# Splitting each attention head's 64 dimensions into even and odd ones instead of lower and upper halves, in a fused attention and maxout kernel

## The chip, the cores and the metric

The kernel runs on one core of one Trainium2 chip. The metric is the device time of one execution in microseconds (us), the median of several. A core has a matrix engine (PE, whose weight loads are listed apart as PEld), a vector engine (DVE), a scalar engine for activation functions (ACT), a general engine (POOL) and a sync engine (SP), which here does nothing but issue transfers. Sixteen DMA engines carry the transfers of the core.

## The reference

```python
def _attn_ref(q, k, v, cap):              # q, k, v: (8, 12, 448, 64)
    scores = matmul(q, k^T) / sqrt(64)
    scores = cap * tanh(scores / cap)     # cap = 30
    attn = softmax(scores)
    return matmul(attn, v)

x = attn_out as (8 * 448 tokens, 12 * 64 = 768)
h1, h2 = x @ w1, x @ w2                   # w1, w2: (768, 1024)
return maximum(h1, h2) @ w_out            # w_out: (1024, 768), result (3584, 768) float32
```

The kernel uses maximum(h1, h2) = relu(x(w1 - w2)) + x w2. So it needs wd = w1 - w2 and the product wm = w2 w_out, and computes relu(x wd) w_out + x wm.

## The kernel before, in words

**Tiling.** 96 heads are taken two at a time ("pairs", 48 of them), and two pairs (four heads) make one step t of 24. Three pairs are one group g for loading, so there are 16 groups. For a step, the scores of each key block go to PSUM (`scores`, lines 297 and 302), ACT takes tanh (lines 303, 305) and exp (`ex`, line 310), PE sums the exponentials for the softmax's divisor (`total`), and PE multiplies them with v (`values`, lines 368 and 375). `values` makes two PSUM tiles, u = 0 and u = 1. In each, the four heads of the step stand in four blocks of 32 partitions, and each block holds one half of that head's 64 dimensions. A weight load for it takes 32 columns of `vp` or `vl` (v in bf16). `normalize` writes the two tiles as rows `2q + u` of xT, where q counts the steps of one batch, so a 128-row chunk of xT holds one half of the dimensions of four heads.

**The weights.** Rows of w1 and w2 must be in the same order as those of xT. The function `x_rows` picks the 128 rows of chunk c: in the kernel before, four blocks of 32 consecutive rows, with 32 rows skipped between blocks. `load_w2(c)` (line 210) brings chunk c of w2 from float32 to bf16 through the queue of POOL into a tile that is named gT in the profile. `load_w1(c)` (line 218) brings chunk c of w1 as float32 (512 KB) through the queue of SP into tiles that the profile names osb (c = 0 to 3) and xT (c = 4, 5). POOL subtracts one from the other (`subtract`, line 221). PE turns chunks of w2 (`turn_w2`, line 228) and multiplies them with w_out (`premultiply`, line 239; chunk 0 by `premultiply_first`, line 527).

**The order of work.** The order on every engine is written out by hand; each engine takes its own list strictly in order. On SP the list begins: k and q of groups 0 and 1, v of group 0, v of group 1, k and q of group 2, w1 chunks 0 and 1, the transposing transfer `cross(2)`, w1 chunks 2 to 5, k and q of group 3, v of group 2, `cross(3)`, and then the later groups. `cross(g)` (line 275) turns the bf16 copies of k and q (kqf) into qkT, which `scores` needs from group 2 on; it has to wait for POOL's casts of that group's k and q (lines 177 to 189). Groups 0 and 1 are turned by PE (`transposes`).

POOL's list in the same stretch: issue w2 chunks 0 and 1 and the four w_out loads (line 201), cast group 1, issue w2 chunks 2 to 5, cast v of groups 0 and 1 (lines 150, 154), cast k and q of group 2, subtract chunks 0 and 1, subtract chunks 2 and 3, cast k and q of group 3, subtract chunks 4 and 5, cast v of group 2.

The two MoE products of each batch (`moe`, lines 403, 415, 418) fill PE between the attention's pieces, through a list of generators from which the function `F(n)` takes n matmuls; the last of them run after the last exp.

[...]

Of the kernel before, what the change touches and what calls it, by code (L numbers as in the profile page):

```python
# [10 lines left out]
def kernel(  # L11
# [11 lines left out]
    nc = tc.nc  # L23
# [5 lines left out]
    B, H, S, D = q.shape  # L29
# [3 lines left out]
    P = 128  # L33
# [30 lines left out]
    vp = [const.tile([P, 2 * L, NJ, D], bf16, name=f"vp{i}") for i in range(2)]  # L64
    vl = [const.tile([P, L, P], bf16, name=f"vl{i}") for i in range(2)]
# [74 lines left out]
    def cast(eng, g, what, n0=0, n1=L, halves=(0, 1)):  # L140
# [53 lines left out]
    w2b = (  # L194
        xpool.tile([P, FC, 2 * S], bf16, name="gT", bufs=1)
        .rearrange("p f s -> p (f s)")[:, : KC * DF]
        .rearrange("p (c n) -> p c n", c=KC)
    )
# [5 lines left out]

    def x_rows(w, c):

        return w.rearrange("(q m u i) n -> q u m i n", m=4, u=2, i=32)[c // 2, c % 2]

    def load_w2(c):
        nc.gpsimd.dma_start(  # L210
            out=w2b[:, c, :], in_=x_rows(moe_w2, c)
        )

    w1x = xpool.tile([P, NP, 2 * S], bf16, name="xT").rearrange("p c s -> p (c s)").bitcast(f32)

    def load_w1(c):
        w1_in[c] = opool.tile([P, DF], f32, name="osb") if c < OB else w1x[:, (c - OB) * DF : (c - OB + 1) * DF]
        nc.sync.dma_start(out=w1_in[c], in_=x_rows(moe_w1, c))
# [29 lines left out]
    expo = {}  # L248
# [63 lines left out]
    def e_of(t, ab, j):  # L312
        p, m = LP[ab, j]
        return expo[t, p][:, m : m + (1 if j == NJ else 2), :]
# [45 lines left out]
    def values(t):  # L360

        out = []
        for u, bank in enumerate(("pv", "ss")):
            ps = pv_psum.tile([P, 512], f32, name=bank)
            for j in range(NJ):
                for ab, h, r in HEADS:
                    g, n = divmod(2 * t + ab, L)
                    nc.tensor.matmul(  # L368
                        ps[r, :S], vp[g % 2][:, 2 * n + h, j, 32 * u : 32 * u + 32], e_of(t, ab, j)[:, h, :],
                        start=(j == 0), stop=False,  # L370
                    )
            for ab, h, r in HEADS:
                g, n = divmod(2 * t + ab, L)
                d = 64 * h + 32 * u
                nc.tensor.matmul(
                    ps[r, :S], vl[g % 2][:, n, d : d + 32], expo[t, 2][:, ab, :], start=False, stop=True
                )
            out.append(ps)
        return out
# [107 lines left out]
    for c in range(2):  # L487
        load_w2(c)
# [21 lines left out]
    for c in range(2, KC):  # L510
        load_w2(c)
# [63 lines left out]
    total(0)  # L575
    F(3)
    normalize(0, values(0))
    F(2)

    for t in range(1, NQ):  # L580
        i = 2 * t
# [55 lines left out]
        else:  # L637
            F(12)
        normalize(t, values(t))
        if t % 3 == 2:  # L640
            fill_q.append(moe(t // 3))
# [35 lines left out]
```

## Time and profile before

| | |
|---|---|
| device time, median of three | 389.99 us (388.97 to 390.05) |
| span of the profiled execution | 388.7 us |
| PE busy | 335.2 us (86%) |
| ACT busy | 281.7 us (72%) |
| DVE busy | 235.0 us (60%) |
| POOL busy | 112.8 us (29%) |
| transfers of SP's queue | 58.21 MB, 55.8% of 16 engines' span |
| transfers of POOL's queue | 3.16 MB, 5.6% |

Busy time is the time in which an engine works on an instruction, and issuing a transfer does not count. A share of the whole span is a mean over stages with different limits: the first 90 us, in which the weights and the first groups come in, are another stage than the steady part up to about 332 us, where the last exp ends, and the tail after it, where PE alone works off the MoE. The lines of the profile are shown where the prediction reads them.

### The profile page before, as it was taken

To read this page: it belongs to the slowest core of one execution; us is meant where nothing else is said; L and a number is where in the kernel's file an instruction comes from. 1 tells how busy PE (TensorE), PEld (TensorE's weight loads), DVE (VectorE), ACT (ScalarE), POOL (GpSimd) and SP (SyncE) were. 2 spreads that over 40 slices of the span, in tenths; PEclk is the share of its full clock that TensorE was granted. 3 is DMA by queue.
4 is the path that set the end of the run, shared out by engine and by line. 5 is a ranking of instruction groups with operands and counts; after the bars stand their busy time and mean duration, and the time that the engine had idled before them with its cause. 6 is when DMAs were issued, how large, how long until landed. Compare 5 with 4: busy or idle time off the path is not lost.

```text
span 388.7 us, 6775 instructions
## 1 busy us (share of the span) xinstructions
PE 335.2 (86%) x2710; PEld 162.6 (42%) x2710; DVE 235.0 (60%) x410; ACT 281.7 (72%) x265; POOL 112.8 (29%) x154
## 2 busy tenths in 40 slices
PE   3387749108899899999999999999999999999996
PEld 1143325004345344444443454444444445455563
DVE  4144507106867786688768876788777677742421
ACT  3679839306899899999999999999999999200000
POOL 5632623174811901370173108111901100000000
PEclk9998969857999999999999999999999999999999
DMA  8999764466986857793978296399268012102022
GB/s 280 212 172 232 115 114 140 144 179 171 271 221 200 233 136 177 232 244 99 258 222 221 58 266 184 107 238 308 83 156 232 2 42 81 42 0 87 37 83 81
DMA packets 105432, 61.80 MB, mean 159 GB/s; under 512 B 64568, under 2 KB 100408, under 8 KB 105400
## 3 DMA queue, kind: packets, MB, share of 16 engines
q1 hardware_dynamic: 101144, 58.21, 55.8%
q0 software_dynamic: 4256, 3.16, 5.6%
q8 instruction: 21, 0.34, 0.4%
q14 instruction: 11, 0.09, 0.1%
HBM read 42.47 MB, written 11.01 MB: 138 GB/s over the span
## 4 chain that ended last, share of the span: by engine, by line
PE 38%; ACT 28%; SPq 11%; DVE 10%; DMA 9%; issue 2%; POOL 1%; ACTq 0%; POOLq 0%
PE mm L403 15%; ACT expo L310 14%; ACT tanh L303 12%; PE mm L418 7%; PE mm L415 5%; SPq L135 4%; DMA gT<-in_moe_w_dram 4%; PE s L302 4%; DVE esum L329 3%; ACT tanh L305 2%; DMA osb<-in_moe_w_dram 2%; DVE esum L331 2%; SPq L124 2%; SPq L129 2%; PE ss L368 2%
## 5 line engine op out<-in xcount | busy, mean ns | idle before, releaser
L303 ACT ACTIVATE tanh<-s 128x896 bf16<-128x896 f32 x144 | 124.2, 914 | 44.2 <-PE s L302 42.3
L310 ACT ACTIVATE expo<-tanh 128x1792 bf16<-128x1792 bf16 (+1 forms) x96 | 144.8, 1509 | 0.1
L418 PE MATMUL mm<-wo_sb,gT 128*128 128x384 bf16 x448 | 86.3, 327 | 0.0
L403 PE MATMUL mm<-xT,wd_sb 128*128 128x448 bf16 x384 | 79.8, 353 | 4.1 <-DVE gT L407 2.4
L302 PE MATMUL s<-qkT 64*128 64x448 bf16 x288 | 43.3, 370 | 32.3 <-DMA qkT<-kqf 26.4
L415 PE MATMUL mm<-wm_sb,xT 128*128 128x384 bf16 x336 | 66.9, 326 | 0.2 <-DVE osb L422 0.2
L157 POOL CAST vp<-vr 128x1152 bf16<-128x1152 f32 x14 | 16.4, 1171 | 141.0 <-PE ss L368 79.1
L418 PEld LDWEIGHTS <-gT 128*128 128x128 bf16 x448 | 42.1, 98 | 35.1 <-issue 8.8
L422 DVE COPY osb<-mm 128x384 f32<-128x384 f32 x56 | 31.0, 554 | 38.2 <-PE mm L418 38.0
L403 PEld LDWEIGHTS <-wd_sb 128*128 128x128 bf16 x384 | 35.9, 98 | 43.5 <-issue 12.9
L331 DVE TENSOR_TENSOR esum<-expo 128x896 bf16<-128x896 bf16 x42 | 30.3, 721 | 29.9 <-ACT expo L310 29.2
L407 DVE TENSOR_SCALAR gT<-mm 128x448 bf16<-128x448 f32 x64 | 39.6, 620 | 13.3 <-PE mm L403 13.0
L415 PEld LDWEIGHTS <-xT 128*128 128x128 bf16 x336 | 31.5, 98 | 26.3 <-issue 6.3
L329 DVE TENSOR_TENSOR esum<-esum,expo 64x896 bf16<-64x896 bf16 x42 | 32.1, 763 | 1.1
L302 PEld LDWEIGHTS <-qkT 64*128 64x128 bf16 x288 | 9.5, 95 | 55.0 <-DMA qkT<-kqf 27.0
L333 DVE TENSOR_TENSOR esum<-esum,expo 128x896 bf16<-128x896 bf16 x42 | 26.8, 638 | 0.2
L305 ACT ACTIVATE tanh<-s 128x896 bf16<-128x896 f32 x24 | 22.0, 917 | 6.5 <-PE s L297 6.0
L244 DVE CAST wm_sb<-mm 128x384 bf16<-128x384 f32 x10 | 5.6, 556 | 33.0 <-PE mm L239 33.0
L354 DVE STREAM_TRANSPOSE st<-ss 128x448 f32<-128x448 f32 x24 | 15.5, 646 | 10.0 <-PE ss L352 5.6
L177 POOL CAST kqf<-kr 128x1152 bf16<-128x1152 f32 x14 | 17.3, 1239 | 12.6 <-DMA kr<-in_k_dram 12.1
L368 PEld LDWEIGHTS <-vp 128*32 128x32 bf16 x576 | 13.3, 96 | 18.5 <-issue 10.7
L368 PE MATMUL ss<-expo,vp 128*32 128x448 bf16 x288 | 17.8, 353 | 1.2 <-DVE st L354 1.1
(69 smaller groups left out, 275.2 us busy)
## 6 DMA issues: line engine op xcount, KB each, us to landing
kr<-in_k_dram SPq DMA_DIRECT2D x14, 576.0 KB, 4.6
qr<-in_q_dram SPq DMA_DIRECT2D x14, 576.0 KB, 8.3
vr<-in_v_dram SPq DMA_DIRECT2D x14, 576.0 KB, 5.3
out_dram<-osb SPq DMA_DIRECT2D x20, 384.0 KB, 2.7
out_dram<-osb SPq DMA_DIRECT2D x16, 192.0 KB, 4.0
osb<-in_moe_w_dram SPq DMA_DIRECT2D x4, 512.0 KB
gT<-in_moe_w_dram POOLq DMA_DIRECT2D x6, 256.0 KB, 13.9
wo_sb<-in_moe_w_out_dram POOLq DMA_DIRECT2D x4, 384.0 KB, 16.2
```

The costliest lines, as they stand in the source:

```text
L302: nc.tensor.matmul(s[:, h, :S], k0[r, j * P : (j + 1) * P], qTn[r, :])
L303: nc.scalar.activation(tanh[t, p][:, 2 * m : 2 * m + 2, :], s[:, :, :S], AF.Tanh, scale=scale / cap)
L305: nc.scalar.activation(tanh[t, p][:, 0:2, :], s[:, :, :S], AF.Tanh, scale=scale / cap)
L310: nc.scalar.activation(expo[t, p], tanh[t, p][:, 0:n, :], AF.Exp, scale=float(cap))
L329: nc.vector.tensor_add(d, d, expo[t, 2][r, :, :])
L331: nc.vector.tensor_add(d, e_of(t, ab, 1 if ab else 0), e_of(t, ab, 2 if ab else 1))
L368: nc.tensor.matmul(ps[r, :S], vp[g % 2][:, 2 * n + h, j, 32 * u : 32 * u + 32], e_of(t, ab, j)[:, h, :], start=(j == 0), stop=False,)
L403: nc.tensor.matmul(ps[:, :S], wd_sb[:, c, f * P : (f + 1) * P], x[:, c, cs], start=(c == 0), stop=(c == KC - 1))
L407: nc.vector.tensor_relu(g[:, f, cs], ps[:, :S])
L415: nc.tensor.matmul(ps[:, : DM // 2], x[:, c, ts], wm_sb[:, c, hs], start=(c == 0), stop=False)
L418: nc.tensor.matmul(ps[:, : DM // 2], g[:, f, ts], wo_sb[:, f, hs], start=False, stop=(f == FC - 1))
L422: nc.vector.tensor_copy(osb[:, hs], ps[:, : DM // 2])
```

## The change

The tile u of a step now holds the dimensions u, u + 2, u + 4 ... of each head, so u = 0 takes the even and u = 1 the odd ones. Chunk c of the weights then consists of every second row of 256 consecutive rows: 128 rows with one constant step of two rows, where before there were four blocks of 32 rows. The purpose is a simpler address pattern for the loads of w1 and w2. In return the 32 columns of v that a weight load takes stand two apart. The sums, the number of instructions and their order on every engine stay what they were.

```diff
     def x_rows(w, c):
 
-        return w.rearrange("(q m u i) n -> q u m i n", m=4, u=2, i=32)[c // 2, c % 2]
+        return w.rearrange("(q p u) n -> q u p n", p=P, u=2)[c // 2, c % 2]
...
                     nc.tensor.matmul(
-                        ps[r, :S], vp[g % 2][:, 2 * n + h, j, 32 * u : 32 * u + 32], e_of(t, ab, j)[:, h, :],
+                        ps[r, :S], vp[g % 2][:, 2 * n + h, j, u::2], e_of(t, ab, j)[:, h, :],
                         start=(j == 0), stop=False,
                     )
...
-                d = 64 * h + 32 * u
                 nc.tensor.matmul(
-                    ps[r, :S], vl[g % 2][:, n, d : d + 32], expo[t, 2][:, ab, :], start=False, stop=True
+                    ps[r, :S], vl[g % 2][:, n, 64 * h + u : 64 * h + 64 : 2], expo[t, 2][:, ab, :], start=False, stop=True
                 )
```

In the built program the source of a w1 or w2 load was 4 x 32 x 1024 elements and is now 128 x 1024; the destination is 128 partitions of 1024 elements in both.

More of the change, by code (lines that the diff above doesn't have):

```diff
@@ L205, in x_rows @@
     def x_rows(w, c):
-        return w.rearrange("(q m u i) n -> q u m i n", m=4, u=2, i=32)[c // 2, c % 2]
+        return w.rearrange("(q p u) n -> q u p n", p=P, u=2)[c // 2, c % 2]
     def load_w2(c):
-        nc.gpsimd.dma_start(
-            out=w2b[:, c, :], in_=x_rows(moe_w2, c)
-        )
+        nc.gpsimd.dma_start(out=w2b[:, c, :], in_=x_rows(moe_w2, c))
     w1x = xpool.tile([P, NP, 2 * S], bf16, name="xT").rearrange("p c s -> p (c s)").bitcast(f32)
```

## The prediction

> **What bounds the kernel now.** I began with the span in 40 slices (9.7 us each), where the first 90 us look different from the rest.
>
> ```profile
> PE   3387749108899899999999999999999999999996
> ACT  3679839306899899999999999999999999200000
> ```
>
> From the tenth slice on PE is at 9 and so is ACT until the tail; before that both fall to 0 or 1 near 78 to 87 us, and sag at 10 to 20 us and 49 us. ACT's timeline gives the three holes with their lengths (last bracket: idle before, and releaser):
>
> ```profile
> 21.40 1.73 ACT L303 ACTIVATE tanh<-s 128x896 bf16<-128x896 f32 x2 [5.02 <-PE s L302]
> ...
> 54.53 1.73 ACT L303 ACTIVATE tanh<-s 128x896 bf16<-128x896 f32 x2 [7.14 <-PE s L302]
> ...
> 89.09 0.92 ACT L303 ACTIVATE tanh<-s 128x896 bf16<-128x896 f32 x1 [17.44 <-PE s L302]
> ```
>
> ACT lost 5.02 + 7.14 + 17.44 = 29.6 us to PE's scores. Next I asked the waits of the first 92 us what PE lacked (total, times, longest):
>
> ```profile
> ACT tanh L303 <- PE s L302: 37.4, 6, 17.4
> ...
> PE s L302 <- DMA qkT<-kqf: 26.4, 2, 18.7
> ...
> POOL wd_sb L221 <- DMA osb<-in_moe_w_dram: 17.7, 4, 9.0
> ...
> POOL kqf L177 <- DMA kr<-in_k_dram: 10.9, 1, 10.9
> ...
> PE mm L228 <- DMA gT<-in_moe_w_dram: 6.2, 1, 6.2
> ```
>
> Hole 1 is chunk 0 of w2 (gT, line 228); holes 2 and 3 are cross(2) and cross(3) (qkT). Behind the crosses stand w1 (osb) and k of group 3. The chain of waits of the same stretch (start, length, what) says the same: w2, w1, then SP's issues, then the last cross.
>
> ```profile
> 5.72 14.07 DMA gT<-in_moe_w_dram
> ...
> 35.63 9.13 DMA osb<-in_moe_w_dram
> ...
> 62.14 8.68 SPq L135
> ...
> 83.85 4.60 DMA qkT<-kqf
> ```
>
> Last, the busy time by windows; the last two columns are the share of the 16 DMA engines and GB/s:
>
> ```profile
> 8.00:10.00 2.00, 1.37 (x26) 0.70 (x25) 1.15 (x3) 2.00 (x3) 2.00 (x4) 1.00 1.06 401
> ...
> 40.00:43.00 3.00, 3.00 (x30) 1.84 (x31) 1.16 (x3) 2.97 (x3) 2.81 (x5) 1.00 0.26 105
> ...
> 55.00:62.00 7.00, 7.00 (x43) 3.85 (x42) 2.37 (x4) 5.92 (x6) 1.07 (x1) 0.84 0.25 100
> 67.00:70.00 3.00, 2.83 (x18) 1.40 (x16) 1.34 (x3) 2.97 (x4) 2.13 (x1) 1.00 0.26 104
> ```
>
> While w1 moves, the share is flat at 0.25 to 0.26, four engines of 16, at 100 to 105 GB/s. At 8 to 10 us, with q, k and v, all 16 worked at 401 GB/s. That plateau is the bound of the start: one 512 KB chunk takes 524 kB / 102 GB/s = 5.1 us, six take 31 us, and everything behind them on those four engines queues.
>
> [...] No strided weight load is in this trace.
>
> **The change part by part.**
>
> w1, six loads (line 218). Each goes from 5.1 us on four engines to 524 kB / about 390 GB/s (near the 401 seen) = 1.35 us, so six go from 31 to 8 us.
>
> w2, six loads (line 210). Chunk 0 was issued at 5.72 and landed at 19.8. On all engines: q, k, v of the first two groups are five loads of 672 KB, 3.44 MB, from about 2 us, hence until 10.8; two chunks of w2 read 1.05 MB, 2.7 us more, so until 13.5[...]. PE asks for it at 13.6, ACT runs dry only at 16.4. Hole 1 closes: ACT and PE move up by 5.0 us. The w_out loads (3.1 MB, 8 us) then run from 13.5 to 21.6; their first lands near 16.5 and is needed at 24.07 - 5 = 19.1, the last is needed at 31 - 5 = 26.
>
> Hole 2. All reads up to q of group 2 are 3.44 + 1.05 + 3.15 + 2.1 (w2 chunks 2 to 5) + 2.06 (v of group 1, k and q of group 2) = 11.8 MB, 30 us at 390 GB/s, so q lands near 33. POOL's last casts of that group take 1.7 us, cross(2) is issued near 36 instead of 43.04, with w1 chunks 0 and 1 (2.7 us) through. Landing costs 4.6 us, the price of the undisturbed cross at 83.85 (this one took 10.8): 40.6. PE reaches it at 46.15 - 5.0 = 41.1. The hole closes; ACT carries on at 47.4 - 5.0 = 42.4 instead of 54.53, 12.1 us earlier.
>
> Hole 3. After cross(2) leaves the engines at about 41, w1 chunks 2 to 5 need 5.4 us, k, q of group 3 another 3.6: landing at 49 and 51. POOL subtracts chunks 2 and 3 by 48 (2.13 us each), casts by 53 (3.65 us in all at 80.20 to 83.83), cross(3) lands at 53.3 + 4.6 = 57.9. PE asks at 69.8 - 12.4 = 57.4; ACT has work until 71.65 - 12.1 = 59.5, and scores take 0.6 us: 58.5. The hole closes with 1 us to spare. ACT's instruction that started at 89.09 starts at about 59.5 to 60.5, a gain of 28.6 to 29.6.
>
> After that nothing is new: the lists are the same, PE and ACT wait for no transfer after 89 us, and the next loads (v of group 3, k and q of groups 4 and 5) follow cross(3) at the same distance as before. So the shift reaches the end. After hole 3 PE ran at a granted clock of 0.50 (window 86 to 90), and ACT then waited 1.81 us at 93.4; a warm PE may return about 1 us. I book it against the risk that a hole leaves a rest.
>
> The strided weights (lines 368, 375): 576 + 192 = 768 loads.
>
> ```profile
> L368 PEld LDWEIGHTS <-vp 128*32 128x32 bf16 x576 | 13.3, 96 | 18.5 <-issue 10.7 <-POOL vp L157 0.4
> ```
>
> A load of 32 columns takes 96 ns, no less than the 98 of the 128-column ones, so 96 ns is not the reading alone; and 12 matmuls follow each other in 0.68 us, 57 ns apart, with loads beside them. Lower bound 0. Upper bound: spacing doubled, 768 x 57 ns = 44 us on PE. I take 0[...].
>
> Sum: 390.0 - 28.5 = 361.5 us.
>
> **The rivals.**
>
> A: w2 does not speed up, since its queue spreads otherwise or because its engines are full in 8 to 20 us (share above 1 there speaks for that). Hole 1 stays at 5.0, holes 2 and 3 close: 390 - 24.5 = 365.5.
>
> B: a new wait takes the old one's place. The chain cross(3) needs subtract, cast and landing in a row, and my slack is 1 us; SP's in-order issues could hold k of group 3. If hole 2 leaves 2 us and hole 3 leaves 7, the time is 361.5 + 9 = 370.5. For it: SP's issues took up to 8.68 us each. Against it: those long issues stand inside the plateau; at 89.90 one took 0.39.
>
> C, the other side: a stride halves the weight load's rate and it shows in full. Then 361.5 + 44 = 405.5, slower than before. Against it: the equal 96 and 98 ns.
>
> D: the plateau has another cause (for instance the rows themselves), loads stay as they are: 390.
>
> **How the numbers follow.** Forecast 0.64, A 0.13, B 0.16, C 0.04, D 0.03. The likeliest gives 361.5. The forecast itself may be off by some 5 us either way (holes with a rest, or the warm clock as an extra gain); A lies inside that, and to hold most of B the range goes to 371. Low end: all 29.6 and about 4 more from the warm clock and from small waits after the holes: 356. Faster by over 0.3%: forecast, A and B, 0.93; same 0.03 (D); slower 0.04 (C).
>
> **What would show it.** Right: DMA share near 1 and 350 GB/s or more while osb is filled; the first gT landing in 7 to 9 us; PE's waits for qkT under 2 us each; ACT without an idle of over 2 us after 16 us; line 368 still at 96 ns and 57 ns apart; the stretch from the first step after cross(3) to the end unchanged in length. Wrong: the plateau at a quarter persists; SP's issues at line 135 stay long; PEld of line 368 above 150 ns, or 12 of its matmuls over 1 us.

## The result, and the profile after

| | before | after |
|---|---|---|
| device time, median (four runs each) | 390.02 us | 365.02 us |
| range | 388.97 to 393.11 | 363.54 to 367.15 |
| span of the profiled execution | 388.7 us | 362.4 us |
| packets of POOL's queue | 4256 | 1952 |

The ratio is 0.9351, 95% interval 0.9278 to 0.9424. The changed kernel takes 25.0 us less. Its lines have other numbers: 300, 301 and 308 are the scores, tanh and exp, 226 and 237 `turn_w2` and `premultiply`, 210 and 216 the loads of w2 and w1, 273 the transposing transfer, 366 and 372 `values`.

The span in 40 slices (9.1 us each) of the changed kernel:

```profile
PE   3898597979999999999999999999999999999996
ACT  3989689979998999899998999999999998000000
```

The hole of two slices is gone. What is left of the three holes stands in ACT's timeline (last bracket: idle before, releaser):

```profile
20.48 1.73 ACT L301 ACTIVATE tanh<-s 128x896 bf16<-128x896 f32 x2 [0.28 <-PE s L300]
24.63 0.92 ACT L303 ACTIVATE tanh<-s 128x896 bf16<-128x896 f32 x1 [0.84 <-PE s L295]
...
44.87 1.73 ACT L301 ACTIVATE tanh<-s 128x896 bf16<-128x896 f32 x2 [3.32 <-PE s L300]
...
49.94 1.73 ACT L301 ACTIVATE tanh<-s 128x896 bf16<-128x896 f32 x2 [1.77 <-PE s L300]
...
62.86 0.92 ACT L301 ACTIVATE tanh<-s 128x896 bf16<-128x896 f32 x1 [0.19 <-PE s L300]
...
66.00 0.92 ACT L303 ACTIVATE tanh<-s 128x896 bf16<-128x896 f32 x1 [0.64 <-PE s L295]
```

The instruction that started at 89.09 starts at 62.86. From it to the end it is 388.7 - 89.09 = 299.6 us before and 362.4 - 62.86 = 299.5 after: all of the gain lies ahead of it. Hole 1 (5.02) is gone, hole 3 (17.44) is 0.19, hole 2 (7.14) is 3.32, and a short wait behind hole 2 grew from 1.08 to 1.77. Before the tanh at 24.63 ACT idles 0.84, where the kernel before has one wait of 0.81 in that stretch, at another tanh. Of the 29.6 us of the three holes, 29.6 - 3.32 - 0.28 - 0.19 - (1.77 - 1.08) - (0.84 - 0.81) = 25.1 us came back. (ACT's first tanh also started 1.1 us sooner in this profile, but it does so in a run below that has the old loads, too, so it isn't the change's.)

The waits of the first 66 us (total, times, longest), and a window in which w1 makes up nearly all that moves (last two columns: share of the 16 DMA engines, GB/s):

```profile
PE s L300 <- DMA qkT<-kqf: 5.9, 2, 4.3
...
POOL wd_sb L219 <- DMA osb<-in_moe_w_dram: 4.2, 1, 4.2
...
POOL kqf L177 <- DMA kr<-in_k_dram: 1.2, 1, 1.2
```

```profile
46.00:49.00 3.00, 3.00 (x11) 1.48 (x10) 0.56 (x1) 2.17 (x2) 1.04 (x1) 0.50 0.98 362
```

PE waited 26.4 us for qkT and waits 5.9; POOL waited 17.7 for w1 and 10.9 for k, now 4.2 and 1.2. The share in the window is 0.98 where it was 0.25, the rate 362 GB/s where it was 100. The chain of waits of that stretch names something new:

```profile
3.69 17.10 DMA vr<-in_v_dram
...
22.76 9.48 DMA vr<-in_v_dram
...
57.71 4.69 DMA qkT<-kqf
```

It no longer goes through w2 and w1 but through v of group 0, the casts that free its buffer, and v of group 1 (issued at 22.76, landed at 32.24).

### The profile page after: what moved, and what is told of

Same layout as the page of the kernel before. It is cut to its first block, busy times and chain, and to the rows that moved or that the text cites. A ratio compares the mean times of both kernels' runs of the same rounds, so it can differ in the third digit from the quotient of the medians.

```text
span 362.4 us, 6775 instructions
## 1 busy us (share of the span) xinstructions
PE 336.7 (93%) x2710; PEld 163.6 (45%) x2710; DVE 237.1 (65%) x410; ACT 281.6 (78%) x265; POOL 113.4 (31%) x154
## 2 busy tenths in 40 slices
DMA packets 103201, 61.79 MB, mean 170 GB/s; under 512 B 62337, under 2 KB 98177, under 8 KB 103169
## 3 DMA queue, kind: packets, MB, share of 16 engines
q0 software_dynamic: 1952, 3.15, 4.8%
## 4 chain that ended last, share of the span: by engine, by line
PE 39%; ACT 28%; DVE 13%; DMA 10%; SPq 4%; POOL 3%; issue 2%; ACTq 0%; POOLq 0%
PE mm L400 15%; ACT expo L308 14%; ACT tanh L301 12%; DMA vr<-in_v_dram 9%; PE mm L415 8%; PE mm L412 6%; PE s L300 3%; DVE esum L327 3%; DVE esum L329 3%; ACT tanh L303 2%; DVE esum L331 2%; PE ss L366 2%; DVE gT L404 2%; PE pv L366 2%; DVE osb L419 1%
## 5 line engine op out<-in xcount | busy, mean ns | idle before, releaser
L329 DVE TENSOR_TENSOR esum<-expo 128x896 bf16<-128x896 bf16 x42 | 31.3, 746 | 29.6 <-ACT expo L308 28.9
L327 DVE TENSOR_TENSOR esum<-esum,expo 64x896 bf16<-64x896 bf16 x42 | 30.5, 727 | 1.1
L331 DVE TENSOR_TENSOR esum<-esum,expo 128x896 bf16<-128x896 bf16 x42 | 29.1, 693 | 0.2
L177 POOL CAST kqf<-kr 128x1152 bf16<-128x1152 f32 x14 | 17.7, 1262 | 3.4 <-DMA kr<-in_k_dram 2.9
L366 PE MATMUL pv<-expo,vp 128*32 128x448 bf16 x288 | 18.1, 356 | 0.0
```

The source lines that it names most:

```text
L327: nc.vector.tensor_add(d, d, expo[t, 2][r, :, :])
L329: nc.vector.tensor_add(d, e_of(t, ab, 1 if ab else 0), e_of(t, ab, 2 if ab else 1))
L331: nc.vector.tensor_add(d, d, e_of(t, ab, 0 if ab else 2))
L366: nc.tensor.matmul(ps[r, :S], vp[g % 2][:, 2 * n + h, j, u::2], e_of(t, ab, j)[:, h, :], start=(j == 0), stop=False,)
```

## The experiments

Two of the edits are in the diff already; where an experiment's edit is short it is shown. Ratios are to the kernel before, run beside it.

**Which load brings how much.** `x_rows` of the changed kernel was used for w1 alone, or for w2 alone, with v as before.

```diff
-        nc.sync.dma_start(out=w1_in[c], in_=x_rows(moe_w1, c))
+        nc.sync.dma_start(out=w1_in[c], in_=x_rows_step(moe_w1, c))
```

> Only w1's loads take the rows in steps of two (w2, v as before, so the rows of w1 and w2 don't belong together). Theory (number of engines): w1 moves at 300 GB/s or more on 16 engines, holes 2 and 3 nearly close, hole 1 (5 us) stays as w2's first chunk still lands at 19 to 20 us: 369 to 371 us. Rival (w1 and w2 both have to be quick, the holes hang on each other): 378 us or more. Rival (w2 never mattered): 365 us.

> Only w2's loads take the rows in steps of two. Theory: first gT landing falls from 14 us to 8 us, hole 1 closes, the plateau of w1 at a quarter of the engines stays with holes 2 and 3; SP's list moves up by some 4 us: 385 to 387 us. Rival (w2 sets the whole start): under 375 us. Rival (w2's queue spreads anyway): 390 us.

Measured: w1 alone 367.70 us, ratio 0.9453 (0.9405 to 0.9501); w2 alone 386.55 us, 0.9928 (0.9892 to 0.9964). Against 389.63 beside them these are 21.9 and 3.1 us (by the intervals 19.4 to 23.2 and 1.4 to 4.2), together 25.0, which agrees with what the whole change brought. ACT's timeline with w1 alone:

```profile
19.30 1.73 ACT L307 ACTIVATE tanh<-s 128x896 bf16<-128x896 f32 x2 [3.66 <-PE s L306]
...
48.22 1.73 ACT L307 ACTIVATE tanh<-s 128x896 bf16<-128x896 f32 x2 [2.54 <-PE s L306]
```

and with w2 alone:

```profile
48.70 1.73 ACT L307 ACTIVATE tanh<-s 128x896 bf16<-128x896 f32 x2 [7.18 <-PE s L306]
...
83.66 0.92 ACT L307 ACTIVATE tanh<-s 128x896 bf16<-128x896 f32 x1 [17.50 <-PE s L306]
```

With w1 alone hole 1 stays (3.66 us) and hole 3 has no line any more; with w2 alone hole 1 has none, and holes 2 and 3 are whole. The first two loads of w2 landed a median 12.9 us after their issue with w1 alone and 8.3 with w2 alone. So each hole belongs to the load that the prediction gave it. The w1 run was 1 to 3 us quicker than its expectation said; its hole 1 was 1.3 us shorter than the 5 us put in, and the rest has no cause shown.

**The strided weights.** Only the two lines of `values` were changed.

> Only the weight loads of v take every second column; w1 and w2 are loaded as before, so the product uses rows in the wrong order. Theory (strided weight loads cost nothing): 390 us within 0.7, line 368's weight loads at 96 ns, 12 matmuls in 0.68 us. Rival (the stride costs PE time that the gain of the loads hides): 393 to 400 us.

Measured: 389.82 us, ratio 1.0001 (0.9978 to 1.0023). Group of the weight loads in this run:

```profile
L366 PEld LDWEIGHTS <-vp 128*32 128x32 bf16 x576 | 13.2, 96 | 18.5 <-issue 10.9
```

That is 96 ns, and its chain of waits has 12 of the matmuls in 0.68 us, as before. Reading every second column costs nothing that these runs can tell from their noise (0.9 us either way); the rival with 3 to 10 us is out.

**Number of engines or the rows themselves.** The rows of before, in the same blocks, but four transfers for each chunk:

```diff
-        nc.sync.dma_start(out=w1_in[c], in_=x_rows(moe_w1, c))
+        for m in range(4):
+            nc.sync.dma_start(out=w1_in[c][32 * m : 32 * m + 32, :], in_=x_rows(moe_w1, c)[m])
```

> The rows of the kernel before, in the same blocks, but each w1 chunk is four transfers of 32 rows to 32 partitions. Theory (the outer dimension of 4 sets the number of engines): each transfer runs on 16 engines, no plateau; as in the run with w1 alone, plus 18 more issues of 0.55 us on SP: 370 to 377 us. Rival (the row addresses, blocks with gaps, are slow): plateau at a quarter stays, 390 us.

Measured: 371.29 us, 0.9536 (0.9495 to 0.9576). A window of its w1 stretch:

```profile
50.00:55.00 5.00, 5.00 (x34) 2.83 (x33) 2.10 (x4) 4.01 (x5) 3.64 (x2) 0.89 1.03 239
```

The share is 1.03: the same rows, in four transfers whose outer dimension is 32, kept all 16 engines busy. The rate is only 239 GB/s, not 362, and why is open: each transfer also fills 32 partitions and not 128, and no run varied that alone. SP's issues come near as a limit, too: its timeline has eight of 131 kB in 3.67 us, which by estimate lets at most 286 GB/s through.

Then the number of blocks, with nothing else changed (`m=8, i=16` and `m=2, i=64` in `x_rows` of before):

> The kernel before with w1 and w2 taken in eight blocks of 16 rows with gaps of 16 (v as before, so the product takes rows in the wrong order). Theory (the outer dimension sets the number of engines): 8 engines, a plateau at half of the DMA engines near 205 GB/s while w1 moves alone, 2.6 us a chunk; 368 to 376 us. Rival (blocks with gaps are slow as such): the quarter stays, 390 us.

> The same with two blocks of 64 rows and gaps of 64. Theory: 2 engines, a plateau at an eighth near 51 GB/s, 10.2 us a chunk, six take 61 us; 415 to 435 us. Rival (longer blocks are better): faster than 390 us.

Measured: 374.97 us with eight (0.9618, 0.9561 to 0.9675), 420.84 with two (1.0795, 1.0759 to 1.083). Windows of the w1 stretch, eight blocks and then two:

```profile
37.00:40.00 3.00, 3.00 (x39) 1.49 (x41) 1.16 (x3) 2.97 (x3) 2.68 (x4) 1.00 0.51 199
```

```profile
66.00:78.00 12.00, 11.80 (x88) 5.71 (x92) 4.43 (x9) 8.98 (x8) 0.11 (x1) 0.76 0.13 47
```

| blocks in the source's outer dimension | share of the engines | GB/s | time, us |
|---|---|---|---|
| 2 | 0.13 | 47 | 420.8 |
| 4 (before) | 0.25 | 100 | 390.0 |
| 8 | 0.51 | 199 | 375.0 |
| 128 rows in one (after) | 0.98 | 362 | 365.0 |

The share is blocks / 16 within 0.02 (the last with 16 of 16), and the time follows. Longer blocks are worse, not better. The time column has w2 in it as well, which is loaded in the same pattern. On POOL's queue no view shows w2's share of the engines, but the waits go the same way: PE's wait for its first chunk was 9.98 us with two blocks, 6.20 with four, 1.15 with eight, and after the change PE's timeline shows none.

**What is left of hole 2.** First the changed kernel once more, as the measure of the three runs beside it:

> The changed kernel once more, as the measure for the three runs beside it: 365 us within 1.5, ACT idle of 3 us before its first tanh after the first transposing transfer (hole 2).

Measured: 363.68 us, 0.9325 (0.9288 to 0.9361). In this profile hole 2 was 1.95 and hole 3 was 2.98 us, against 3.32 and 0.19 in the first: together they came to 3.5 us in the first and 4.9 us in the second. POOL's timeline of the first profile shows what the transposing transfer (issued at 39.48) stood behind:

```profile
32.30 1.37 POOL L150 CAST vp<-vr 64x576 bf16<-64x576 f32 x2 [9.56 <-DMA vr<-in_v_dram]
...
35.84 1.14 POOL L177 CAST kqf<-kr 128x1152 bf16<-128x1152 f32 x1
```

v of group 1 landed at 32.3, its casts took until 35.8, and only then came those of k and q. So v got a second raw buffer (`bufs=2`), which lets it be issued at 4 us instead of 23:

> The changed kernel with two raw buffers for v, so that v of group 1 is issued at about 4 us and not behind the casts of group 0's v (23 us before). Theory (the rest of hole 2 is v of group 1, late because its buffer is held, and its casts ahead of those of k and q on POOL): the first transposing transfer is issued by 34 us and not at 39.5, hole 2 under 1 us, w_out a little later: 361 to 363.5 us. Rival (the engines are full until 33 us, so an earlier issue only moves others back): 365 us or more, with PE waiting for w_out.

Measured: 362.94 us, 0.9313 (0.9277 to 0.935), no different from the changed kernel. POOL's timeline:

```profile
33.81 1.14 POOL L177 CAST kqf<-kr 128x1152 bf16<-128x1152 f32 x1 [3.63 <-DMA kr<-in_k_dram]
...
36.35 1.15 POOL L177 CAST kqf<-qr 128x1152 bf16<-128x1152 f32 x1 [0.70 <-DMA qr<-in_q_dram]
```

v is out of the way, but POOL now waits for k until 33.81 and for q until 36.35; the transposing transfer went out at 38.09, 1.4 us sooner than in the first profile of the changed kernel, and hole 2 was 2.35. The time lies in the range that the theory gave, but its reason fell: the issue was to come by 34 us and hole 2 to go under 1 us. The rival's reason was the better one in part, though PE lost only 0.56 us to w_out. k of group 2 was issued at 8.24, 15 us sooner than in the changed kernel (23.22), and still came only at 33.8. In the changed kernel all 16 engines are busy in that stretch (a share of 1.03 to 1.16 in every 2 us from 10 to 34 us): here the bytes ahead counted more than the time of issue. For q there is a second possible reason, which no run tells from the first: SP's two issues before it took 13.2 us, so it was itself issued only at 21.98.

```profile
8.65 13.22 SPq L135 DMA_DIRECT2D kr<-in_k_dram  x2
21.98 2.81 SPq L124 DMA_DIRECT2D qr<-in_q_dram  x1
```

The next runs take 1 MB out of the front (w2 chunks 4 and 5 are first used near 49 us); the second of them also loads and casts k and q of group 2 ahead of v of group 1:

```diff
-    for c in range(2, KC):
+    for c in range(2, 4):
         load_w2(c)
...
     cast(nc.gpsimd, 2, "k")
     cast(nc.gpsimd, 2, "q")
+    for c in range(4, KC):
+        load_w2(c)
```

> The changed kernel with w2 chunks 4 and 5 issued after POOL's casts of group 2 (about 39 us and not 18), 1 MB less on the engines in front of v of group 1 and k, q of group 2. Theory (transfers in front are what delays v of group 1): it lands 2 to 2.5 us sooner, hole 2 shrinks by as much: 362 to 363.5 us. Rival (that landing is set by its late issue alone): 365 us.

> As the run with late w2 chunks, and also k and q of group 2 loaded and cast before v of group 1. Theory: the first transposing transfer waits only for k and q, is issued near 30 us and lands long before PE asks; but v of group 1 is cast later, and the values of step 1 may wait for it by up to 3 us: 361 to 364 us. Rival (w_out, which shares the engines with the earlier k and q, arrives late and costs PE more than hole 2): 366 us or more.

Measured: 368.45 us (0.9445, 0.9413 to 0.9478) and 367.59 us (0.9452, 0.9411 to 0.9494), both slower than the changed kernel. Both forecasts of a gain were missed. In the run with late w2 chunks alone the theory held as far as it went: v of group 1 was cast from 28.53, and the transfer issued at 35.71, 3.8 us sooner. But then, in PE's timeline of the run with late w2 chunks:

```profile
50.59 0.93 PE L300 MATMUL s<-qkT 64*128 64x448 bf16 x4 [9.90 <-DMA qkT<-kqf]
```

and its DMA issues from 35 us on (issue to landing):

```profile
gT<-in_moe_w_dram POOLq DMA_DIRECT2D x2, 256.0 KB, 9.3
...
qkT<-kqf SPq DMA_TRANSPOSE x1, 14.8
```

The transposing transfer took 14.8 us (15.6 in the other run) beside the two w2 loads, and 4.7 in the changed kernel. (The other run's 367.59 lies where its rival put it, but w_out cost PE only 1.8 us there, against 9.2 for qkT.) To test that these two are what slowed it, they were moved behind it, and w1 chunks 4 and 5 behind k and q of group 3:

```diff
             subtract(0, nc.gpsimd)
             subtract(1, nc.gpsimd)
+            for c in range(4, KC):
+                load_w2(c)
...
-    for c in range(2, KC):
+    for c in range(2, 4):
         load_w1(c)
     load(3, "k")
     load(3, "q")
+    for c in range(4, KC):
+        load_w1(c)
```

> The changed kernel with w2 chunks 4 and 5 issued after POOL's subtraction of chunks 0 and 1 (so after the first transposing transfer has landed, unlike the run with late w2 chunks), and w1 chunks 4 and 5 loaded after k and q of group 3. Theory (late w2 failed only because its two loads ran beside the transposing transfer): v of group 1 lands near 28.5 as there, the transposing transfer is issued near 36 and takes 4.7 us, hole 2 falls under 1 us, hole 3 stays under 1 us: 359 to 361.5 us. Rival (the transposing transfer took 14.8 us there because it was issued earlier, beside w1 chunks 0 and 1): it takes 10 us or more again, 365 us or more.

> As the run before in this call, with two raw buffers for v as well. Theory: v of group 1 is then no longer what the first transposing transfer waits for, k and q of group 2 are; issued near 35 us: within 1 us of that run.

Measured: 362.82 us (0.9313, 0.9281 to 0.9345) without and 360.92 us (0.9252, 0.9217 to 0.9287) with the second buffer. The first can't be told from the changed kernel. The transposing transfer took 6.1 and 6.3 us though it was issued at 36.70 and 34.96, as early as where it took 14.8, and with w1 chunks 0 and 1 ahead of it as there: the w2 loads beside it were the cause. (w1 chunks 4 and 5 were moved in the same runs, but in the first 6.9 us of the slow transfer SP had issued nothing behind it yet, and it had not landed.) The w2 loads were not wholly out of its way even now, as they went out 4.2 us after its issue, at 40.93 and 39.20. Without the second buffer the forecast of 359 to 361.5 was missed. Hole 2 was 2.01, hole 3 was 1.93 (its transposing transfer took 7.0 us), and PE then waited for the late w2 chunk itself:

```profile
48.06 0.40 PE L226 MATMUL mm<-ident,gT 128*128 128x128 bf16 x2 [2.31 <-DMA gT<-in_moe_w_dram]
```

With the second buffer the time was to be within 1 us of the run without; it was 1.9 us less. ACT's timeline has this left:

```profile
41.78 1.73 ACT L301 ACTIVATE tanh<-s 128x896 bf16<-128x896 f32 x2 [1.22 <-PE s L300]
46.62 1.73 ACT L301 ACTIVATE tanh<-s 128x896 bf16<-128x896 f32 x2 [1.53 <-PE s L300]
...
60.03 0.92 ACT L301 ACTIVATE tanh<-s 128x896 bf16<-128x896 f32 x1 [0.70 <-PE s L300]
```

This is the fastest kernel of the study. Its interval against before (0.9217 to 0.9287) ends where that of the changed kernel in its second measurement (0.9288 to 0.9361) begins, and overlaps that of the first (0.9278 to 0.9424), so it is probably quicker than the change alone by 2 to 3 us; the two were never run side by side.

## Why the prediction was right, and where its sum was off

The 365.0 us lie in the range, 3.5 us above the likeliest value. That they lie next to rival A's 365.5 is chance: A has hole 1 open and hole 2 closed; here hole 1 closed and hole 2 kept a rest.

Three steps of the prediction were shown by no trace when it was made and were the author's estimates: that a load with one constant step of rows uses all 16 engines, that this holds for POOL's queue as for SP's, and that a step of two columns costs the weight loads nothing. The runs bear out what they were to bring: a share of 0.98 for w1, the first w2 loads landed 8.3 us after issue with w2 alone (12.9 with w1 alone), and 96 ns a weight load.

- **w1 on 16 engines: right, and shown.** The share follows the number of blocks over four values (0.13, 0.25, 0.51, 0.98), and with four transfers of the old rows it is full (1.03), so rival D is out. The rate was 362 GB/s where 390 was put in, 1.45 us a chunk and not 1.35.
- **w2: right, and shown; its worth was put too high.** The first loads of w2 landed 8.4 us after issue (7 to 9 forecast), and hole 1 closed but for 0.28 us (0.98 in the second profile), so rival A is out. How long a load takes to land behind its last byte no view shows; that the sum had chunk 0 there in time was the author's estimate. By itself w2 was worth 3.1 us (1.4 to 4.2), where 5.0 were booked for hole 1.
- **Hole 2: closed only in part, as the sum followed the wrong transfer.** The step that failed is "q lands near 33 ... cross(2) is issued near 36 instead of 43.04": it was issued at 39.48. PE's longest wait for qkT was 4.3 us, where under 2 was to be the sign of being right. Two terms were wrong. The first is the path: the "1.7 us" of casts after q left out that POOL casts in the order v, k, q. v of group 1, issued at 22.76 when the casts of group 0 had freed its buffer, landed at 32.24, and from there POOL worked through 3.5 us of v and 3.6 us of k and q without waiting. The lines of the kernel before had the same order, and its v landed late as well (POOL cast it from 35.86). The second is the rate: the 11.8 MB ahead don't come at 390 GB/s. In the changed kernel q was issued at 27.38 and took 8.1 us to land, so it was there at 35.5, not 33; with a second buffer for v it was there by 36.35, which for 11.8 MB in 34.3 us is 344 GB/s on average. (That is an estimate; w1's first bytes moved beside them, and q's own issue at 21.98 may have had a part.) With both removed (second buffer, 1 MB less ahead) the issue came at 34.96. In the first profile this hole's 3.32 us are the bulk of the 3.5 us by which 361.5 fell short of 365.0; in the second, hole 3 has the larger rest.
- **The clock: the gain came where it was put, and was lost elsewhere.** About 1 us was expected back after hole 3, where the kernel before had a wait of 1.81 us behind a granted clock of 0.50. That wait is now 0.64 (the last line of ACT's timeline above), and the windows from 62 to 68 us have a clock of 1.00. Later waits took it back (the one of 1.75 at 107.33 is now 2.18 at 80.36), as the whole stretch to the end is as long as before. And hole 2 didn't close, and PE had the lower clock behind it: the window 34 to 36 us, ahead of the hole, shows 1.00, the window 46 to 49 us shows 0.50, and 14 matmuls of line 237 took 4.36 us there, where 13 of them took 2.28 before the hole. ACT's next wait was 1.77 us, 1.08 in the kernel before.
- **Hole 3: nearly closed, with luck in the timing.** The transposing transfer landed at 57.71 + 4.69 = 62.4 us, 4.5 us later than the sum's 57.9. Hole 3 stayed at 0.19 us because ACT, held up at hole 2, had work until 62.7 and not 59.5. The second profile shows 2.98 us. The rests of holes 2 and 3 are rival B on a small scale.
- **The rest unchanged, the stride free: right, and shown**, by 299.6 against 299.5 us and by the ratio of 1.0001. Rival C is out.

## What to carry to other kernels

Look at the share of DMA engines while one transfer moves alone: a flat level at a simple fraction (0.25 with four blocks) meant here that its access pattern, not its bytes, set the rate, and a view of rows as few blocks with gaps was such a pattern; with one constant step the same bytes moved at 0.98. It can pay to move the pattern to a place where it costs nothing, as the step of two in the weight loads did here (96 ns as before, ratio 1.0001). After such a fix, ask what stands in order behind the transfer that got faster: here a cast queue (3.5 us of v's casts) and the bytes ahead (11.8 MB) were next, and two loads moved out of the way came to lie beside a transposing transfer, which then took 14.8 us instead of 4.7.

## What was not expected of the hardware

- A transposing transfer beside two loads on POOL's queue took 14.8 and 15.6 us. It took 4.7 and 5.4 without them, and 6.1 and 6.3 where they went out 4.2 us after it; beside w1 at a share of 0.25, in the kernel before, 10.8. Which of their properties does it (the casting, the queue, the full engines) was not tried.
- The packets of POOL's queue depend on the blocks, though its bytes hardly do. The queue's lines (packets, MB, share) with two blocks, and of the kernel after:

```profile
q0 software_dynamic: 7328, 3.17, 4.9%
```

```profile
q0 software_dynamic: 1952, 3.15, 4.8%
```

With eight blocks there were 2720, with four 4256. Per w2 load that is 128, 384 and 896 more than with one step, or 128 x (16 / blocks - 1); they are small ones: the packets under 512 B of the whole kernel are 62337 after the change and 67628 with two blocks.
